# Attention feeding a routed mixture of experts: a new issue order, two packed parameter loads, and the first expert's weight parts moved behind the last route

## The chip, the cores and the metric

The kernel runs on 1 core of one Trainium2 chip. The metric is device time in microseconds (us) of one execution; lower is better. Before the change it is 464.62 us, the median of 3 runs (464.45 to 464.82).

## The reference

Inputs: q, k, v of shape (2 batches, 8 heads, 768 tokens, 64), a hash matrix of 64 x 6, and the experts' weights (8 experts, 512 x 1024 and 1024 x 512).

```
q_bucket, k_bucket = 6 sign bits of q@proj, k@proj, as a number
mask   = q_bucket[:, None] == k_bucket[None, :]
scores = where(mask, q@k.T / 8, -1e9)
attn   = exp(scores - max) / (sum + 1e-9);   x = attn @ v        # (2, 768, 8*64)

for b: for s in order:
    fresh = argmax(x[b,s] @ w_gate)
    e = fresh if s == 0 or sigmoid(x[b,s] @ w_local) < 0.5 else previous e
    p = softmax(x[b,s] @ w_gate)[e]
    out[b,s] = p * (relu(x[b,s] @ w1[e]) @ w2[e])
```

The expert of a token can depend on the token before it, so routing is a scan along the sequence.

## The kernel before

Engine names are those of the profile: PE multiplies matrices, DVE, ACT and POOL work elementwise, SP only starts transfers; POOL and ACT start some too.

**Attention.** Heads go in 8 pairs, p = 0 to 7; pairs 0 to 3 are batch 0. A pair has 12 units `s1` (128 queries by 384 keys: PE products, then a maximum on DVE, L222), which give the row maxima, and 12 units `s2` (128 keys by 384 queries: four products on PE, L213, then exp on ACT, L263, to a tile `pt`). `pv` multiplies `pt` with v (L277), `padd` sums `pt` over key blocks on DVE or POOL (L270). `hash` and `bd` make the bucket bits and put them into the tiles `b` as extra rows; `hi` and `lo` split q and k into a rounded part and the rest (`hx`, `lx`). `ma` to `mf` put the maxima in. `sa`, `sb` (`sah`, `sbh` for half a pair) make the divisors, `ot` copies the result out of PSUM, and `ug` turns it by a product with `iw`, an identity with gate weights beside it (L371), and divides it (L379, L384).

**The order.** `ORDER` is a list written out by hand: each word calls one of these functions, and all engines keep this order within their own queues. `MOVED` says which units sit on a second engine or queue. `busy` is a pair of products on zeros whose result nobody reads. `vsum`, `flat` serve rows whose bucket is empty.

**Routing.** `route` (called through `step`, in parts) runs once for batch 0, then for each half of batch 1. It finds the expert (DVE, L438 to L445, result `rZ`), turns it (PE, L455, tile `tk`), scans along the tokens (DVE, L458, L460), turns the result back (L467, tile `tb`), computes each token's slot `rsi` and probability (L473 to L488), and lets POOL write the tokens' rows into `xs`, a table in DRAM of 256 slots for each expert (L494). Expert 0's inputs don't wait for the table: `xt0` is put together in PSUM by products with one-hot matrices (`oh`, L580; `gather`, L614), from rows read back for batch 0 (`xa`, L588) and from the rounded and rest parts `xhl` of batch 1's first half and `xh`, `xl` of its second half.

**Experts.** `expert` (eight times) loads four parts of w1 and four of w2 of 512 KB each through SP (L644, four buffers `st`), splits each into a rounded part `wh` (ACT, L647) and a rest `wl` (L648), and multiplies (L678, tile `hps`; L696, tile `yps`), three products for each pair. `wl` is made by DVE, for the four w1 parts of expert 0 by POOL. `xprep` loads the next expert's rows `xsl` (L653) and turns them (L657, tile `xps`); `PI` (L629) holds the probabilities and token numbers of expert 0. `overflow_count` counts experts with more than 256 tokens.

Of the kernel before, what the change touches and what calls it, by code (L numbers as in the profile page):

```python
# [22 lines left out]
lx.0.0 busy.2 lx.0.1 busy.2 busy.2 busy.2 lhw busy.2 busy.2 hi.0.1 busy.2 lcs busy.2 lx.1.0 lx.1.1 busy.2 busy.2  # L23
hash.0 hi.0.0 busy.2 ident busy.2 bd.0.1.1 busy.2 hi.1.1 lo.0.1 bd.0.0.1 lo.0.0 busy.2 bd.0.0.0 bd.0.1.0 busy.2
load_v.0.2 busy.2 busy.2 busy.2 hash.1 busy.2 busy.2 s1.0.0.0 busy.2 s1.0.0.1 s1.0.1.0 hi.1.0 lo.1.0 busy.2 lx.2.1
busy.2 s1.0.1.1 bd.1.0.0 busy.2 bd.1.0.1 s1.0.2.0 busy.2 s1.0.2.1 busy.2 busy.2 clear busy.2 busy.2 load_v.0.0
s1.0.3.0 ma.0.0 busy.2 s1.0.3.1 busy.2 busy.2 busy.2 bd.1.1.1 busy.2 mb.0.0 s1.0.4.0 busy.2 lx.2.0 load_v.0.3 s1.0.4.1
s1.0.5.0 bd.1.1.0 busy.2 s1.0.5.1 busy.2 busy.2 mc.0.0 lo.1.1 s2.0.1.0 ma.0.1 s2.0.0.0 s1.1.0.0 hash.2 mb.0.1 busy.2
s1.1.0.1 busy.2 s1.1.1.0 s2.0.2.0 s1.1.1.1 busy.2 load_v.0.5 load_v.0.1 s1.1.2.0 hi.2.1 s2.0.4.0 load_v.0.4 lx.3.0
mf.0.0 mc.0.1 s2.0.3.0 s1.1.2.1 busy.2 s2.0.1.1 bd.2.1.0 s1.1.3.0 s2.0.0.1 busy.2 s1.1.3.1 s2.0.4.1 s1.1.4.0 bd.2.1.1  # L30
busy.2 padd.0.1.0 s2.0.2.1 bd.2.0.1 s1.1.4.1 vsum.0 hi.2.0 s2.0.5.1 s1.1.5.0 s1.1.5.1 pv.0.0.0 bd.2.0.0 mf.0.1
pv.0.1.0 padd.0.1.1 pv.0.0.1 pv.0.1.1 s1.2.0.0 s2.0.5.0 s2.0.3.1 s1.2.0.1 s1.2.1.0 pv.0.2.0 padd.0.2.0 ma.1 lx.3.1 iwc
pv.0.2.1 hash.3 io flat.0.1 flat.0.0 mb.1 s1.2.1.1 padd.0.3.0 padd.0.2.1 s1.2.2.0 s1.2.2.1 hi.3.1 bd.3.0.0 bd.3.0.1
pv.0.3.0 pv.0.3.1 pv.0.4.1 hi.3.0 padd.0.3.1 lo.2.0 padd.0.4.1 mc.1 bd.3.1.1 padd.0.4.0 pv.0.4.0 pv.0.5.1 bd.3.1.0
s1.2.3.0 s2.1.1.0 padd.0.5.1 s2.1.0.0 s1.2.3.1 padd.1.1.0 s2.1.2.0 s2.1.2.1 s1.2.4.0 s2.1.1.1 padd.0.5.0 s2.1.0.1
s2.1.3.0 lo.2.1 s2.1.5.0 s1.2.4.1 padd.1.2.0 lx.4.0 mf.1 pv.0.5.0 s1.2.5.0 padd.1.1.1 s1.2.5.1 s1.3.0.0 ot.0
padd.1.2.1 pv.1.0.1 pv.1.0.0 pv.1.1.0 pv.1.2.0 s1.3.0.1 s2.1.5.1 padd.1.3.0 s2.1.4.1 s1.3.1.0 s2.1.4.0 lx.4.1 s2.1.3.1
load_v.1.3 ma.2 s1.3.1.1 sa.0 padd.1.3.1 hash.4 flat.1.1 flat.1.0 mb.2 sb.0 pv.1.1.1 pv.1.2.1 bd.4.1.0 lo.3.0 pv.1.3.0
pv.1.3.1 padd.1.4.1 s1.3.2.0 s1.3.2.1 lx.5.0 s1.3.3.0 pv.1.4.1 bd.4.0.0 bd.4.0.1 pv.1.4.0 mc.2 pv.1.5.1 pv.1.5.0
s1.3.3.1 hi.4.1 iwl.1 ot.1 s2.2.0.0 padd.1.4.0 s2.2.1.1 s1.3.4.0 lo.3.1 bd.4.1.1 padd.1.5.0 s2.2.2.1 iwl.0 s2.2.1.0  # L40
padd.1.5.1 s1.3.4.1 s1.3.5.0 lx.5.1 pv.2.0.0 s1.3.5.1 s2.2.3.0 hi.4.0 s2.2.3.1 s2.2.2.0 s2.2.0.1 s2.2.4.0 sa.1 ma.3
padd.2.1.0 hash.5 mb.3 padd.2.1.1 sb.1 padd.2.2.0 mc.3 pv.2.0.1 pv.2.1.1 pv.2.1.0 pv.2.2.0 mf.2 pv.2.2.1 s1.4.0.0
# [734 lines left out]
```

## Time and profile before

| | |
|---|---|
| time, median of 3 | 464.62 us (464.45 to 464.82) |
| profiled execution: its own time, its span | 463.13 us, 461.3 us |
| PE busy | 432.1 us, 94% |
| DVE, ACT, POOL busy | 297.3, 203.3, 177.2 us |
| DMA | 60.17 MB, mean 130 GB/s |
| granted PE clock, mean of the span | 0.983 |

Busy time of PE includes ends that are modelled, so a PE that is busy need not run at its peak; what tells is the idle time before an instruction and who ended it (in brackets in the rows below). Span and time differ by what lies before and after the program's instructions. The attention with its routing takes the first 271 us of the span, the experts the rest.

### The profile page before, as it was taken

The page shows a single profiled execution, that of the slowest core. Times are in us where ns is not written, and L with a number is a line of the kernel's source. Part 1 is how long each engine was busy: PE and PEld are TensorE (multiplying, and loading weights), DVE is VectorE, ACT ScalarE, POOL GpSimd, SP SyncE. Part 2 cuts the span into 40 slices and gives each one's busy share as a digit, 9 for nine tenths or more (in the row PEclk, how much of TensorE's full clock was granted, in tenths as well). Part 3 has the DMA queues.
Part 4 walks back from the last instruction along what each step waited for, and adds up shares of the span by engine and source line. Part 5 has one row for each costly group of instructions (what it writes and reads, how often), then busy time and mean ns, then how long its engine had stood idle before and what let it go on. Part 6 is the DMA issues. An engine that isn't in the chain of part 4 may idle for free.

```text
span 461.3 us, 8283 instructions
## 1 busy us (share of the span) xinstructions
PE 432.1 (94%) x3316; PEld 338.3 (73%) x3316; DVE 297.3 (64%) x441; ACT 203.3 (44%) x277; POOL 177.2 (38%) x127
## 2 busy tenths in 40 slices
PE   8989999999999999999988289999999999999993
PEld 7976565765767475566654289899999999998982
DVE  5987794646675768876678977573736473738210
ACT  1133454552726353353355046473736364646210
POOL 4369455388577566165356620101010101010100
PEclk9999999999999999999999599999999999999997
DMA  4532111112040030501156539966766766775000
GB/s 154 158 105 76 51 60 42 43 31 81 1 153 28 2 107 3 184 0 70 48 190 222 182 113 285 327 210 217 230 220 219 219 240 220 234 233 192 36 2 31
DMA packets 41577, 60.17 MB, mean 130 GB/s; under 512 B 5949, under 2 KB 24093, under 8 KB 41536
## 3 DMA queue, kind: packets, MB, share of 16 engines
q1 hardware_dynamic: 38010, 50.54, 34.1%
...
HBM read 47.66 MB, written 11.56 MB: 128 GB/s over the span
## 4 chain that ended last, share of the span: by engine, by line
PE 41%; issue 36%; DVE 12%; POOL 5%; ACT 3%; DMA 2%; POOLq 0%; SPq 0%; DVEq 0%; ACTq 0%
PE s L213 19%; PE pv L277 11%; POOL out L700 4%; PE ug L371 3%; DVE rw L438 3%; PE busy L550 2%; DVE sp L270 2%; ACT pt L263 2%; DVE mx L222 2%; PE hb L181 1%; DMA PI<-xs 1%; DVE lx L205 1%; DMA hw<-proj 1%; DVE rC L460 1%; PE pv L284 1%
## 5 line engine op out<-in xcount | busy, mean ns | idle before, releaser
L222 DVE TENSOR_REDUCE mx<-s 128x2 f32<-128x768 f32 x96 | 88.5, 953 | 41.2 <-PE s L213 40.6
L648 DVE TENSOR_TENSOR wl<-st,wh 128x1024 fp32r<-128x1024 f32 x60 | 71.9, 1220 | 60.7 <-ACT wh L647 60.7
L263 ACT ACTIVATE pt<-s 128x768 f32<-128x768 f32 x96 | 73.2, 811 | 64.8 <-PE s L213 59.6
L270 POOL TENSOR_TENSOR sp<-sp,pt 128x768 f32<-128x768 f32 x42 | 79.5, 1904 | 57.1 <-DVE sp L270 28.7
L647 ACT ACTIVATE wh<-st 128x1024 fp32r<-128x1024 f32 x64 | 66.6, 1059 | 49.3 <-DMA st<-w 29.2
L213 PE MATMUL s<-hx 64*128 64x384 f32 x384 | 71.1, 366 | 3.0 <-DVE mx L222 2.7
L678 PE MATMUL hps<-xH,wh 128*128 128x256 f32 x256 | 70.8, 278 | 0.7 <-ACT xH L711 0.7
L678 PE MATMUL hps<-xH,wl 128*128 128x256 f32 x256 | 70.6, 277 | 0.0
L678 PE MATMUL hps<-xL,wh 128*128 128x256 f32 x256 | 70.4, 277 | 0.0
L700 POOL DMA_INDIRECT out<-y,xsl x14 | 15.3, 1092 | 143.3 <-ACT y L699 143.3
L277 PE MATMUL pv<-pt,v 128*64 128x384 f32 x384 | 68.5, 494 | 0.0
L213 PE MATMUL s<-b,b 64*128 64x384 f32 x384 | 65.1, 334 | 0.0
L213 PEld LDWEIGHTS s<-hx 64*128 64x128 f32 x384 | 36.2, 184 | 26.1 <-issue 8.8
L696 PE MATMUL yps<-wh,hH 128*128 128x512 f32 x128 | 50.6, 395 | 0.0
L696 PE MATMUL yps<-wh,hL 128*128 128x512 f32 x128 | 50.4, 393 | 0.0
L696 PE MATMUL yps<-wl,hH 128*128 128x512 f32 x128 | 50.0, 391 | 0.0
L277 PEld LDWEIGHTS pv<-pt,v 128*64 128x64 f32 x384 | 24.9, 136 | 32.9 <-issue 32.1
L678 PEld LDWEIGHTS hps<-xH,wh 128*128 128x128 f32 x256 | 48.1, 188 | 1.2 <-ACT xH L711 0.9
L678 PEld LDWEIGHTS hps<-xH,wl 128*128 128x128 f32 x256 | 48.1, 188 | 0.3
L678 PEld LDWEIGHTS hps<-xL,wh 128*128 128x128 f32 x256 | 48.0, 188 | 0.0
L213 PEld LDWEIGHTS s<-b,b 64*128 64x128 f32 x384 | 36.4, 185 | 0.4 <-DMA b<-br 0.4
L213 PE MATMUL s<-hx,lx 64*128 64x384 f32 x192 | 32.6, 334 | 0.0
...
## 6 DMA issues: line engine op xcount, KB each, us to landing
...
```

Of the source, the lines that this page charges most:

```text
L213: nc.tensor.matmul(out=sc[:, h, 0:384], lhsT=w[r, cols[0]], rhs=x[r, cols[1]], tile_position=(64 * h, 0), start=first and n == 0, stop=las ...
L222: nc.vector.tensor_reduce(out=MX[p][:, kh, i // 3, :, i % 3], in_=sc[:, :, 0:384], axis=AX.X, op=ALU.max)
L263: nc.scalar.activation(out=pt.rearrange("p (a q) -> p a q", a=2), in_=sc[:, :, 0:384], func=ACTF.Exp, scale=0.125)
L270: eng.tensor_tensor(out=SP[p, h], in0=PT[p, 0, h] if kt == 1 else SP[p, h], in1=PT[p, kt, h], op=ALU.add)
L277: nc.tensor.matmul(out=PV[p][64 * h:64 * h + 64, half, 0:384], lhsT=V[b, kt][:, pp * 128 + 64 * h:pp * 128 + 64 * h + 64], rhs=PT[p, kt, h ...
L371: nc.tensor.matmul(out=t[:, half, j * 146:j * 146 + 146], lhsT=OT[p][:, q * 128:q * 128 + 128], rhs=iw[:, pp])
L438: V_.scalar_tensor_tensor(out=kp, in0=LG[b][:, qr, 8], scalar=0.0, in1=cs[:, 160 + q0:160 + q0 + n], op0=ALU.is_ge, op1=ALU.mult)
L647: nc.scalar.activation(out=H, in_=st, func=ACTF.Copy)
L648: (eng or nc.vector).tensor_tensor(out=L, in0=st, in1=H.bitcast(F32), op=ALU.subtract)
L678: nc.tensor.matmul(out=hps[:, k], lhsT=w[:, c, fs], rhs=x[:, c], start=(n == 0), stop=(n == 11))
L696: nc.tensor.matmul(out=yps, lhsT=h[:, k, ts], rhs=w[:, k], start=(n == 0), stop=(n == 23))
L700: i = nc.gpsimd.indirect_dma_start(out=out, out_offset=bass.IndirectOffsetOnAxis(ap=pi[:, t, 1:2].bitcast(I32), axis=0), in_=y, in_offset= ...
```

## The change

- `ORDER` and `MOVED` are replaced. The units are the same, but 40 words `busy` stand where 44 stood, and their order on every engine is another. Two of the differences that matter below: of the first four loads of q and k, three go out at once (SP: xq, xk; ACT: xk of pair 1), and the fourth, xq of pair 1, goes on SP behind `hw` and `cs`; and two more `s2` units of pair 7 stand ahead of the first half's `ugh`.
- `hw` (hash matrix) and `iw` come ready-made from DRAM, in one load each, in place of a memset and two or three loads.
- The last part of the attention (the gathers of `xt0`) is issued by hand as well; `hle` makes both of its rests on DVE.
- The first expert's `wl` are made by DVE, not by POOL, and held behind the route: the first one behind the last one-hot matrix, the others behind the route's last copy. Its `wh` on ACT are held behind the route's last copy `rK`.
- `overflow_count` is issued after expert 0, and `xsl` of expert 1 is loaded by POOL's queue.

```
-lx.0.0 busy.2 lx.0.1 busy.2 busy.2 busy.2 lhw busy.2 busy.2 hi.0.1 busy.2 lcs busy.2 lx.1.0 ...
+busy.2 busy.2 lx.0.0 lx.0.1 busy.2 busy.2 busy.2 lhw lcs lx.1.0 hi.0.1 lo.0.1 lx.1.1 hi.0.0 ...
...
-            nc.scalar.activation(out=K, in_=tk[0:8, i, 0:384], func=ACTF.Copy)
+            AFTER["ACT"] = nc.scalar.activation(out=K, in_=tk[0:8, i, 0:384], func=ACTF.Copy).ins
...
-        V_.tensor_copy(out=EC[b][:, :, qr], in_=tb...)
+        AFTER["last"] = V_.tensor_copy(out=EC[b][:, :, qr], in_=tb...).ins
...
-    nc.vector.memset(hw, 0.0)
...
     def lhw():
-        for h in range(2):
-            queue("lhw").dma_start(out=hw[64 * h:64 * h + 64, 13 * h:13 * h + 12]...
+        queue("lhw").dma_start(out=hw, in_=proj)
...
-        nc.gpsimd.memset(iw, 0.0)
...
-    def iwl(h): ...
-    def iwc(): ...
+    def iwl():
+        nc.sync.dma_start(out=iw.rearrange("p a c -> p (a c)"), in_=wg)
...
     def onehot(tag, o):
-            nc.vector.tensor_scalar(out=oh[:, j], in0=IO[0], ...)
+            AFTER["first"] = nc.vector.tensor_scalar(out=oh[:, j], in0=IO[0], ...).ins
...
     def hle(i):
-        (nc.gpsimd, nc.vector)[i].tensor_tensor(
+        nc.vector.tensor_tensor(
...
-    overflow_count()
...
-    def weights(src, shape, pool, eng=None):
+    def weights(src, shape, pool, after=None):
...
-        nc.scalar.activation(out=H, in_=st, func=ACTF.Copy)
-        (eng or nc.vector).tensor_tensor(out=L, in0=st, in1=H.bitcast(F32), op=ALU.subtract)
+        with tc.issue_after(after["ACT"]) if after else nullcontext():
+            nc.scalar.activation(out=H, in_=st, func=ACTF.Copy)
+        with tc.issue_after(after.pop("first", after["last"])) if after else nullcontext():
+            nc.vector.tensor_tensor(out=L, in0=st, in1=H.bitcast(F32), op=ALU.subtract)
...
-    def xprep(slots):
+    def xprep(slots, queue=nc.sync):
...
     for e in range(NE):
-        xt = expert(w1[e], w2[e], xt, (lambda: xprep(...)) ..., None if e else nc.gpsimd)
+        xt = expert(w1[e], w2[e], xt, (lambda: xprep(..., nc.sync if e else nc.gpsimd)) ..., None if e else AFTER)
+        if e == 0:
+            overflow_count()
```

POOL, from the rows of batch 0 (`xt_109`) written to the slots to the load of `PI`, before; `xl` are rests of batch 1's second half:

```order
L494 DMA xs<-xt_109,rsi 2048x514 x6
L356 TENSOR_TENSOR xl<-xt_110,xh 128x3x128 x3
L494 DMA xs<-xt_110,rsi 2048x514 x3
L595 TENSOR_TENSOR xhl<-xt_110,xhl 128x768
L648 TENSOR_TENSOR wl<-st,wh 128x1024 x4
L494 DMA xs<-xt_110,rsi 2048x514 x3
L629 DMA PI<-xs 128x2x2
```

and now (L623 is `PI`, L648 is now `xsl`):

```order
L356 TENSOR_TENSOR xl<-xt_110,xh 128x3x128
L270 TENSOR_TENSOR sp<-sp,pt 128x768
L356 TENSOR_TENSOR xl<-xt_110,xh 128x3x128
L494 DMA xs<-xt_109,rsi 2048x514 x6
L494 DMA xs<-xt_110,rsi 2048x514 x3
L356 TENSOR_TENSOR xl<-xt_110,xh 128x3x128
L494 DMA xs<-xt_110,rsi 2048x514 x3
L623 DMA PI<-xs 128x2x2
L648 DMA xsl<-xs 128x2x514
```

The rest `xhl` and the four `wl` have left POOL, the three `xl` are spread, and `xsl` stands behind `PI`.

DVE, from the last copy back (`ec`) of the last route on, before (`RK` feeds the one-hot matrices; `OV`, `ni`, `bt` belong to `overflow_count`):

```order
L470 COPY ec_121<-tb 128x24
L510 COPY OV<-to 128x17
L471 TENSOR_TENSOR RK<-tb,ec_121 128x3
L473 TENSOR_TENSOR rt_3101<-tb,cs 128x24
L580 TENSOR_SCALAR oh<-io,RK 128x256 x3
L474 SCALAR_TENSOR_TENSOR rt_3101<-rt_3101,tb 128x24
```

and now, with the first `wl` (L643) behind the one-hot matrices (L573):

```order
L470 COPY ec_121<-tb 128x24
L471 TENSOR_TENSOR RK<-tb,ec_121 128x3
L573 TENSOR_SCALAR oh<-io,RK 128x256 x3
L473 TENSOR_TENSOR rt_3079<-tb,cs 128x24
L643 TENSOR_TENSOR wl<-st,wh 128x1024
L474 SCALAR_TENSOR_TENSOR rt_3079<-rt_3079,tb 128x24
```

DVE, from the last sum of the last route into the first expert, before, where the two halves of `xL` (L712) take rests of w2 between them:

```order
L516 TENSOR_REDUCE bf_3232<-bt_3231 1x5
L487 TENSOR_TENSOR xt_110<-rpr,rse 128x3
L517 CAST be<-bf_3232 1x5
L712 TENSOR_TENSOR xL<-xt_3113,xH 128x512
L648 TENSOR_TENSOR wl<-st,wh 128x1024
L712 TENSOR_TENSOR xL<-xt_3113,xH 128x512
L648 TENSOR_TENSOR wl<-st,wh 128x1024 x3
```

and now, where the first half of `xL` (L707) stands inside the route and the second behind the second `wl`:

```order
L486 TENSOR_REDUCE rpr<-rt_3080 128x3
L707 TENSOR_TENSOR xL<-xt_3091,xH 128x512
L487 TENSOR_TENSOR xt_110<-rpr,rse 128x3
L488 COPY ec_121<-tb 128x2x24
L491 COPY cnt_3187<-rC 8x1
L643 TENSOR_TENSOR wl<-st,wh 128x1024
L707 TENSOR_TENSOR xL<-xt_3091,xH 128x512
L643 TENSOR_TENSOR wl<-st,wh 128x1024 x3
```

The column `xt_110` that L487 writes is what the last three writes to the slots (L494) wait for. On PE the first expert's products start now with eight of the first w1 part, then seven of the second, and only then those that read the second half of `xL`.

## Rows read from the trace of the kernel before

**Rows 1.** Busy time by stretch: window, PE, PEld, DVE, ACT, POOL, clock, DMA, GB/s.
```profile
22.00:45.00 23.00, 21.62 (x207) 16.44 (x203) 18.57 (x26) 9.13 (x12) 16.85 (x13) 1.00 0.29 90
45.00:70.00 25.00, 23.87 (x201) 15.37 (x201) 21.95 (x27) 10.68 (x15) 12.40 (x7) 1.00 0.16 51
145.00:170.00 25.00, 24.21 (x202) 15.53 (x201) 16.30 (x28) 11.59 (x17) 16.46 (x12) 1.00 0.14 49
170.00:195.00 25.00, 23.06 (x198) 15.65 (x196) 20.52 (x34) 10.42 (x15) 11.64 (x7) 1.00 0.24 87
245.00:270.00 25.00, 14.46 (x97) 11.30 (x92) 21.48 (x51) 6.84 (x11) 15.19 (x9) 0.80 0.45 159
285.00:461.00 176.00, 168.37 (x1099) 152.42 (x1097) 89.39 (x91) 84.47 (x105) 17.58 (x16) 0.99 0.58 190
```
**Rows 2.** DVE in order of time, L438: start, duration, idle before in brackets.
```profile
233.93 0.15 DVE L438 SCALAR_TENSOR_TENSOR rw<-lg,cs 128x3 f32<-128x3 f32 x1
...
250.28 10.67 DVE L438 SCALAR_TENSOR_TENSOR rw<-lg,cs 128x3 f32<-128x3 f32 x1
```
**Rows 3.** POOL in order of time, the same stretch.
```profile
250.00 1.75 POOL L595 TENSOR_TENSOR xhl<-xt,xhl 128x768 fp32r<-128x768 f32 x1
251.69 9.23 POOL L648 TENSOR_TENSOR wl<-st,wh 128x1024 fp32r<-128x1024 f32 x4
```
**Rows 4.** PE in order of time, from the last route to expert 0's turn of xsl.
```profile
261.97 0.80 PE L455 MATMUL tk<-cs,rZ 128*8 128x128 f32 x3 [9.30 <-DVE rZ L445]
...
271.32 0.38 PE L678 MATMUL hps<-xH,wh 128*128 128x256 f32 x1 [0.75 <-ACT xH L711]
...
282.75 1.04 PE L657 MATMUL xps<-cs,xsl 128*128 128x128 f32 x8
```
**Rows 5.** Busy time by stretch, around that wait (columns of rows 1).
```profile
250.00:262.00 12.00, 2.39 (x20) 1.98 (x19) 11.93 (x10) 1.69 (x3) 10.92 (x5) 0.69 0.45 158
262.00:266.00 4.00, 4.00 (x25) 3.70 (x25) 3.32 (x10) 0.48 (x1) 0.00 (x0) 0.66 0.37 129
```
**Rows 6.** Chain of waits, the start: start, duration, what held it.
```profile
2.46 4.71 DMA hw<-proj
```
**Rows 7.** PE in order of time, the start.
```profile
1.78 5.36 PE L550 MATMUL busy<-Fl 64*128 64x384 f32 x40 [1.78 <-DVE Fl L538]
```
**Rows 8.** DVE and POOL in order of time, pair 7's second half.
```profile
235.34 3.75 DVE L270 TENSOR_TENSOR sp<-pt 128x768 f32<-128x768 f32 x1 [0.29 <-ACT pt L263]
239.20 0.96 DVE L270 TENSOR_TENSOR sp<-sp,pt 128x768 f32<-128x768 f32 x1
...
235.60 2.67 POOL L356 TENSOR_TENSOR xl<-xt,xh 128x384 fp32r<-128x384 f32 x3
```
**Rows 9.** Chain of waits: two s2 units on PE.
```profile
29.38 1.39 PE s L213 x16
```
**Rows 10.** DVE in order of time, the last route and expert 0's xL.
```profile
266.33 0.18 DVE L470 COPY ec<-tb 128x24 f32<-128x24 f32 x1 [0.17 <-PE tb L467]
...
266.80 0.15 DVE L471 TENSOR_TENSOR RK<-tb,ec 128x3 f32<-128x3 f32 x1
...
271.30 0.69 DVE L712 TENSOR_TENSOR xL<-xt,xH 128x512 fp32r<-128x512 f32 x1 [2.23 <-ACT xH L711]
```
**Rows 11.** Costliest groups of instructions: busy, mean ns, idle before.
```profile
L648 DVE TENSOR_TENSOR wl<-st,wh 128x1024 fp32r<-128x1024 f32 x60 | 71.9, 1220 | 60.7 <-ACT wh L647 60.7
```
**Rows 12.** POOL in order of time, the last writes to the slots and PI.
```profile
271.84 0.97 POOL L494 DMA_INDIRECT xs<-xt,rsi  x1 [0.30 <-issue]
276.53 0.76 POOL L629 DMA_DIRECT2D PI<-xs  x1 [3.72 <-DMA xs<-xt,rsi]
```
**Rows 13.** Chain of waits: from PI's issue to its landing.
```profile
276.53 5.13 DMA PI<-xs
```
**Rows 14.** The tile xsl: from issue to landing, all seven loads by SP.
```profile
DMA to landing us min/median/max: 2.5/3.3/7.0
```
**Rows 15.** Busy time by stretch, while POOL issues PI (columns of rows 1).
```profile
274.00:278.00 4.00, 4.00 (x36) 4.00 (x35) 4.00 (x5) 2.38 (x4) 0.76 (x1) 1.00 0.67 168
```

More of the change, by code (lines that the diff above doesn't have):

```diff
@@ L1 @@
-from contextlib import ExitStack
+from contextlib import ExitStack, nullcontext
 import numpy as np
@@ L22 @@
 ORDER = """
[L23 to L42, printed above, removed]
@@ L68 @@
-pv.7.2.1 padd.7.3.1 s2.7.4.1 s2.7.5.1 step split_l.2 split_l.0 xa.1 split_l.1 flat.7.1 step hle.0 hle.1 pv.7.3.1
-sah.7.1 pv.7.4.1 ohe pv.7.5.1 oth.7.1 sbh.7.1 ugh.7.1 split_h.3 step split_l.3
+busy.2 busy.2 lx.0.0 lx.0.1 busy.2 busy.2 busy.2 lhw lcs lx.1.0 hi.0.1 lo.0.1 lx.1.1 hi.0.0 busy.2 busy.2 hash.0
+busy.2 busy.2 load_v.0.1 bd.0.0.1 busy.2 hi.1.1 bd.0.1.0 ident lo.0.0 busy.2 busy.2 bd.0.0.0 busy.2 lo.1.1 bd.0.1.1
+busy.2 busy.2 hash.1 hi.1.0 busy.2 busy.2 lx.2.0 lx.2.1 busy.2 busy.2 s1.0.0.0 busy.2 bd.1.1.1 load_v.0.3 s1.0.0.1
@@ L599, in tile_kernel @@
     parts = {f.__name__: f for f in (
-        bd, busy, clear, fill_slots, fill_some, flat, hash, hi, hle, ident, io, iwc, iwl, lcs, lhw, lo, load_v, lx,
+        bd, busy, clear, fill_slots, fill_some, flat, hash, hi, hle, ident, io, iwl, lcs, lhw, lo, load_v, lx,
         ma, mb, mc, mf, ohe, ot, oth, padd, pv, s1, s2, sa, sah, sb, sbh, split_h, split_l, step, ug, ugh, vsum, xa)}
-    with tc.manual_schedule():
-        for part in ORDER.split():
-            part, *where = part.split(".")
-            parts[part](*map(int, where))
-    xt0 = pvp.tile([128, 4, 256], F32, tag="pv", name="xt0")
-    x2 = xt0.rearrange("p (b c) n -> p b (c n)", b=2)
-    for i in range(2):
-        nc.tensor.matmul(out=x2[:, i], lhsT=zr, rhs=Fl[0:1, 0:512], start=True, stop=False)
     def gather(oh, hl, c0, c1, last=False):
@@ L662, in xprep, with expert @@
         return xsl[:, :, 512:514], xH, xL
-    def expert(w1e, w2e, xt, mid=None, eng=None):
+    def expert(w1e, w2e, xt, mid=None, after=None):
         pi, xH, xL = xt
@@ L667, in expert @@
         w2v = w2e.rearrange("(f p) c -> p f c", p=128)
-        W1 = [weights(w1v[:, :, 256 * i:256 * i + 256], [128, 4, 256], w1p, eng) for i in range(4)]
+        W1 = [weights(w1v[:, :, 256 * i:256 * i + 256], [128, 4, 256], w1p, after) for i in range(4)]
         hs = []
@@ L759 @@
     B, H, S, D = inputs["q"].shape
+    hw, iw = np.zeros((128, 32), np.float32), np.zeros((128, 4, 146), np.float32)
+    g = np.concatenate([inputs["moe_w_gate"], inputs["moe_w_local"]], axis=1).reshape(4, 2, D, 9)
+    iw[:, :, 0:128] = np.eye(128)[:, None]
+    for h in range(2):
+        r = slice(64 * h, 64 * h + 64)
+        hw[r, 13 * h:13 * h + 12] = np.tile(inputs["proj"], (1, 2))
+        iw[r, :, 128 + 9 * h:137 + 9 * h] = g[:, h].transpose(1, 0, 2)
     arrays = {
```

127 lines of the change are left out of this document (74 added, 53 removed), and 8 rows, old and new, of the table MOVED.

## The prediction, made before the run

> **What bounds the kernel now.** I read four views, in this order. The busy times by stretch say which engine has no room: the reader is to see that PE has idle time of only 1.38 us in the stretch from 22 to 45 us, 1.13 from 45 to 70, 0.79 from 145 to 170 and 1.94 from 170 to 195, and then, all at once, some ten of 25 us from 245 on [rows 1]. From 285 us to the end PE is busy 168.4 of 176 us; it is the bound of the experts, so whatever starts them later or makes PE wait in them moves the end by as much [rows 1]. The second view, PE in order of time, names the gap: PE waits 9.30 us for DVE's `rZ` of the last route, and expert 0 starts at 271.32 us [rows 4]. The third, DVE in order of time, says why: one small instruction of the route (L438) took 10.67 us, where the same one took 0.15 us a route earlier [rows 2]. The fourth, POOL in order of time, says whom it waited for: it began 0.28 us after POOL had begun `xhl`, POOL then ran the four `wl` without a pause, and both ended together (251.69 + 9.23 = 260.92 and 250.28 + 10.67 = 260.95 us) [rows 2, 3]. DVE had waited for POOL's elementwise work on SBUF, not for data. In the same gap the granted clock fell: 0.69 and 0.66 in the means of the next stretches, that is the lower level of 1.2 GHz for part of them [rows 5].
>
> **The change part by part.** The sum is made against the profiled execution's own 463.13 us, which is 1.49 us under the median of 464.62.
>
> *The wait at L438.* With `xhl` and the four `wl` off POOL, nothing but one short `xl` and transfers' issues are left there. The instruction should take 0.15 us again: gain 10.5 us. If POOL's remaining `xl` (a third of 2.67 us [rows 8]) falls upon it, 0.9 us of that are lost.
>
> *The clock.* Without the long gap I expect the full 2.4 GHz. At 0.66 of it, PE's `tk` took 0.80 us [rows 4, 5] and should take some 0.5; with a little for the gathers I count 0.5 us gained (bounds 0 and 1).
>
> *overflow_count.* Its copies stood on DVE between the scan and the one-hot matrices: `RK` began 0.47 us after `ec` [rows 10], with one of them in between. 0.4 us gained; they now stand among expert 0's rests of weights, where DVE has waits to spare [rows 11].
>
> *The first `wl` on DVE.* Here the change costs something, since DVE is now on the way into expert 0. Call X the moment when the first half of `xH` is ready (271.3 before). Before, all of `wl` was there, and 96 products ran from 271.32 to 282.75 without a gap, 0.119 us each [rows 4]. Now DVE makes the first `wl` (1.22 us [rows 11]) while PE gathers, which hides it; but behind it come ten small instructions of the route, so the first half of `xL` ends at about X + 1.0, not X + 0.7 (its own 0.69 us [rows 10]). PE's first eight products end at X + 1.7. The seven of the second part need the second `wl`: X + 1.0, three small instructions of 0.15 us each, 1.22 us, together X + 2.7; PE is through with them at X + 3.5, the second half of `xL` is there at X + 3.4, and the other 81 products take 9.6 us: X + 13.1 in place of X + 11.4. Loss 1.7 us (bounds 0.7, if the route's instructions fit before X, and 3).
>
> *`xsl` behind `PI` on POOL.* PE turns it right after those 96 products. The last three writes to the slots wait for L487, which now stands behind the first half of `xL`: X + 1.2, and with the lag to POOL X + 1.5. They are issued 1.27 us apart (0.97 and 0.30 [rows 12]), the last at X + 4.0. From the last one's issue to `PI` it was 4.69 us [rows 12], so `PI` is issued at X + 8.7 and `xsl` at X + 9.5. SP's loads of it landed after 2.5 to 7.0 us [rows 14], `PI` itself on POOL's queue after 5.1 [rows 13]. Nearest is `PI`; for 514 KB in place of 2 KB I take 6 us: X + 15.5 against X + 13.1, so PE waits 2.4 us (bounds 0 and 3.5). Nothing later gives it back, since PE has no slack there [rows 1]. While POOL issued `PI`, DVE was busy 4.00 of 4 us and the issue took 0.76 us [rows 12, 15]: it was not held up visibly.
>
> *The start.* The first hash product waited 4.71 us for `hw` [rows 6], which queues behind 384 KB loads; four of these were under way, now three are ahead of it. A quarter of 4.71 is 1.2 us. PE has 28 products on zeros ahead of the hash, not 40, at 5.36/40 us each [rows 7]: 1.6 us less, so they don't stand in the way. I take 1.1 us (bounds 0 and 1.6).
>
> *Pair 7's second half.* DVE's first sum took 3.75 us where the next took 0.96, beside three `xl` of 2.67 us on POOL [rows 8]: the same wait as at L438, on the way to the scan. The `xl` are spread now: gain 2.8 us. Against it two more `s2` units stand before the first half's `ugh`: 1.39 us [rows 9]. Net 1.4 us (bounds -1.5 and 2.8). The six writes of batch 0's rows to the slots come later, and `xa`, read back from them, with them; I expect it just in time and keep 1.5 us of the lower bound for it.
>
> *The rest of the order.* PE work is the same but for 16 products on zeros. What a new order can win is PE's idle time in the four stretches above, 1.38 + 1.13 + 0.79 + 1.94 = 5.2 us; it can also lose. I take 1.5 us, some three tenths, with bounds of 5.2 on both sides. This is the least certain term. The ready-made `iw` takes loads off SP and a memset off POOL, far from where they are used: nothing.
>
> Sum: 10.5 + 0.5 + 0.4 - 1.7 - 2.4 + 1.1 + 1.4 + 1.5 = 11.3 us. 463.13 - 11.3 = 451.8 us for an execution like the profiled one, and with 1.49 us back, 453.3 us for the median.
>
> **The rivals.**
>
> *Late `xsl` and a slow clock.* If `xsl` lands at its upper bound, or POOL's issue of it is held up by DVE's `wl`, PE waits 3.5 us or more, and the clock may fall, as in the 9.30 us gap [rows 4, 5]. What the two stretches of rows 5 lost to the clock, 0.31 x 12 + 0.34 x 4 = 5.1 us of full speed, is its price if PE is busy all that time. Against it: shorter gaps went without a fall (clock 1.00 in the stretches from 22 to 195 us [rows 1]), and `PI`'s issue was not held up. 453.3 + 1.1 + 5.1 = 459.5 us. The Trainium skill, SBUF — State Buffer, section "SBUF: two separate sides", warns of just this pair: a transfer issued from GpSimd can be starved of descriptors while VectorE runs an instruction in a two-port mode, 620 ns becoming some 3100 by its figures. By that rule alone, without the clock, `xsl` would land some 2.5 us later and the result would be an estimated 456 us; the 0.76 us of `PI`'s issue beside a busy DVE speak against it.
>
> *The order wins more.* The idle time of the four stretches goes nearly all (3.7 us more than counted) and `xsl` is in time (2.4): 447.2 us. For it: PE's waits there are short and many, which is what an order can mend; against it: any order has DVE reduce, ACT exponentiate and PE multiply the same units.
>
> *Weights late.* The buffers `st` came free when POOL made `wl`, by 260.9 us, X - 10 [rows 3]; now the last one comes free at about X + 6.7, and the fourth part of w2 is loaded only then. At 190 GB/s [rows 1] 512 KB take 2.8 us, rounding and rest 2.3 more: X + 11.8, before its use. If loads crowd and take twice as long, the whole of expert 0 and 1 runs behind them by some 5 us: 458 us.
>
> *Slower than before.* DVE's sums and splits of two SBUF tiles wait whole POOL instructions out, as the 2.8 us in rows 8. The units move, and POOL's and DVE's shares stay alike, so such meetings will come at other places. Where they hit the maxima of `s1`, for which PE waits, each costs PE up to 2.8 us. Five more than now in pairs 1 to 6 eat the gain (5 x 2.8 = 14 against 11.3); with five the time is 453.3 + 14 = 467 us. Against it: there are about as many such sums and splits on either engine as before, so that many more meetings on PE's way would be chance.
>
> *It does not do what it says.* Another instruction of POOL holds L438, or the route waits elsewhere for as long: 464.6 us.
>
> **How the numbers follow.** Forecast 0.55 (453.3 us, own range 450 to 456.5); order wins more 0.15; late `xsl` with slow clock 0.15; weights late 0.08; no effect 0.03; slower 0.04. About 0.2% (0.9 us) is what a measurement of this kernel can tell from no change. Faster: 0.55 + 0.15 + 0.15 + 0.08 = 0.93; same 0.03; slower 0.04. The range reaches from 448 to 459.5 us; outside lie the slower cases, the one without effect and part of the fastest.
>
> **What would show it.** Right: L438 under 1.2 us in the last route; no PE wait over 2 us for `rZ`; clock 1.00 around it; the first hash product near 6.2 us; expert 0's first product near 261 us. For the costs: two waits of PE in its first 15 products, for `xL` and for the second `wl`, and one of about 2.4 us before `xps`. Wrong: DVE again in one small instruction for microseconds while POOL runs; expert 0 starting at 261 us but the end not earlier by as much, with waits for `wh` or `wl`; or PE idle in pairs 1 to 6 by more than the 5.2 us of before.

## The result, and the profile after

The changed kernel takes 458.43 us (median of 4 runs, 458.17 to 461.59) against 464.72 us; the ratio is 0.9877 (95% interval 0.9851 to 0.9904). That is faster, as forecast, but by 6.3 us where 11.3 were forecast. The time lies inside the stated range (448 to 459.5 us) and outside the forecast's own (450 to 456.5 us). Two rivals stand near it, "weights late" (458 us) and "late `xsl` and a slow clock" (459.5 us): the time alone does not tell them apart, the trace has to.

| | before | after |
|---|---|---|
| profiled execution: own time, span | 463.13, 461.3 us | 458.60, 456.8 us |
| PE busy | 432.1 us | 431.3 us |
| DVE, ACT, POOL busy | 297.3, 203.3, 177.2 us | 284.7, 205.6, 171.9 us |
| X, first half of `xH` ready | 271.3 us | 253.6 us |
| first product of expert 0, of expert 1 | 271.3, 294.6 us | 254.6, 289.0 us |

Expert 0 starts 16.7 us earlier, expert 1 only 5.7 us. The busy times by stretch (columns as in [rows 1]) show where:

```profile
22.00:45.00 23.00, 21.53 (x199) 16.27 (x201) 15.25 (x22) 11.86 (x16) 12.29 (x9) 1.00 0.21 61
45.00:70.00 25.00, 25.00 (x218) 15.92 (x215) 18.97 (x29) 13.90 (x21) 18.18 (x10) 1.00 0.29 95
145.00:170.00 25.00, 25.00 (x209) 15.69 (x210) 17.31 (x29) 10.58 (x15) 11.13 (x9) 1.00 0.08 22
170.00:195.00 25.00, 25.00 (x216) 17.33 (x216) 18.79 (x29) 11.50 (x16) 21.55 (x12) 1.00 0.02 4
245.00:270.00 25.00, 17.64 (x147) 16.80 (x144) 18.28 (x37) 12.66 (x16) 10.07 (x8) 0.96 0.80 254
270.00:285.00 15.00, 9.93 (x41) 8.45 (x42) 8.89 (x10) 8.12 (x10) 1.02 (x2) 0.72 0.83 285
285.00:457.00 172.00, 163.79 (x1075) 148.42 (x1073) 83.76 (x89) 78.68 (x98) 16.61 (x16) 0.99 0.55 179
```

In the three stretches between 45 and 195 us that are shown, PE's idle time (1.13, 0.79 and 1.94 us before) is gone; from 22 to 45 us it is 1.47 us, where it was 1.38. The gap now lies between 245 and 285 us, where DMA moves 254 to 285 GB/s and the clock falls to a mean of 0.72. DVE in order of time, the last route, answers [rows 2]:

```profile
242.57 0.15 DVE L438 SCALAR_TENSOR_TENSOR rw<-lg,cs 128x3 f32<-128x3 f32 x1
...
246.85 1.58 DVE L460 TENSOR_TENSOR_SCAN rC<-rE,rC 8x384 f32<-8x384 f32 x1
```

L438 takes 0.15 us and comes 7.7 us earlier. PE in order of time answers [rows 4]:

```profile
244.77 0.49 PE L455 MATMUL tk<-cs,rZ 128*8 128x128 f32 x3
...
254.62 0.36 PE L673 MATMUL hps<-xH,wh 128*128 128x256 f32 x1 [1.75 <-DVE cnt L491]
...
275.07 1.94 PE L652 MATMUL xps<-cs,xsl 128*128 128x128 f32 x8 [9.20 <-DMA xsl<-xs]
```

The wait of 9.30 us for `rZ` is gone, and one of 9.20 us for `xsl` has come. What `xsl` waited for stands on POOL (answers [rows 12]):

```profile
254.64 1.89 POOL L494 DMA_INDIRECT xs<-xt,rsi  x1 [7.03 <-DVE cnt L491]
256.83 3.68 POOL L494 DMA_INDIRECT xs<-xt,rsi  x1 [0.31 <-issue]
260.82 0.97 POOL L494 DMA_INDIRECT xs<-xt,rsi  x1 [0.30 <-issue]
268.76 0.76 POOL L623 DMA_DIRECT2D PI<-xs  x1 [6.97 <-DMA xs<-xt,rsi]
269.50 0.77 POOL L648 DMA_DIRECT2D xsl<-xs  x1
```

and DVE beside it:

```profile
254.45 1.20 DVE L643 TENSOR_TENSOR wl<-st,wh 128x1024 fp32r<-128x1024 f32 x1
255.58 0.67 DVE L707 TENSOR_TENSOR xL<-xt,xH 128x512 fp32r<-128x512 f32 x1
256.19 3.47 DVE L643 TENSOR_TENSOR wl<-st,wh 128x1024 fp32r<-128x1024 f32 x3
259.59 0.67 DVE L678 SCALAR_TENSOR_TENSOR hL<-hps,hH 128x512 fp32r<-128x512 f32 x1
```

The writes of tokens' rows to the slots (L494, `DMA_INDIRECT`) are called scatters from here on, and the making of a `wl` a split. The first two scatters end 0.88 and 0.85 us after the `wl` beside them end (255.65 and 259.66 us). The third, with no split beside it, takes 0.97 us as before. The list of DMA issues gives the median us from issue to landing, here of one transfer each (the third scatter, and the load of `xsl`):

```profile
xs<-xt,rsi POOLq DMA_INDIRECT x1, 7.7
xsl<-xs POOLq DMA_DIRECT2D x1, 514.0 KB, 5.4
```

Before, the last scatters landed 3.2 to 5.0 us after their issue. A held scatter was in the trace of before as well, between two that were not held: one of the first half's began while DVE made the rest `xhl` and ended 0.84 us after it.

```profile
246.90 0.96 DVE L595 TENSOR_TENSOR xhl<-xt,xhl 128x768 fp32r<-128x768 f32 x1 [1.23 <-ACT xhl L594]
...
247.13 1.57 POOL L494 DMA_INDIRECT xs<-xt,rsi  x1 [0.30 <-PE pv L277]
```

X, the end of the first `xH`, is read from ACT, before and after:

```profile
270.67 0.60 ACT L711 ACTIVATE xH<-xt 128x512 fp32r<-128x512 f32 x1 [7.38 <-PE xt L614]
...
252.97 0.60 ACT L706 ACTIVATE xH<-xt 128x512 fp32r<-128x512 f32 x1 [0.37 <-PE xt L599]
```

The wait for `xsl` hides a second bound. ACT and DVE make `hH` and `hL` for the products behind it, and splits that waited for loads stand among these: the fourth part of w2 is rounded only from 267.06 us on, and its `wl` ends at X + 15.8, where the prediction had X + 11.8. Two parts of expert 1's w1 follow. So the last `hL` that expert 0 needs ends at 273.2 us, 1.9 us before PE goes on:

```profile
267.06 1.06 ACT L641 ACTIVATE wh<-st 128x1024 fp32r<-128x1024 f32 x1 [1.95 <-DMA st<-w]
...
272.52 0.68 DVE L678 SCALAR_TENSOR_TENSOR hL<-hps,hH 128x512 fp32r<-128x512 f32 x1
```

### The profile page after: what moved, and what is told of

The parts are those of the page before. It is cut to its first block, busy times and chain, and to the rows that moved or that the text cites. A ratio compares the mean times of both kernels' runs of the same rounds, so it can differ in the third digit from the quotient of the medians.

```text
span 456.8 us, 8266 instructions
## 1 busy us (share of the span) xinstructions
PE 431.3 (94%) x3300; PEld 337.6 (74%) x3300; DVE 284.7 (62%) x445; ACT 205.6 (45%) x278; POOL 171.9 (38%) x121
## 4 chain that ended last, share of the span: by engine, by line
PE 52%; issue 38%; POOL 5%; DVE 2%; DMA 1%; ACT 1%; POOLq 0%; SPq 0%; ACTq 0%
PE s L213 23%; PE pv L277 15%; POOL out L695 4%; PE busy L549 4%; PE ug L371 3%; PE hb L181 1%; PE st L329 1%; POOL xs L494 1%; PE xt L599 1%; PE pv L284 1%; PE st L338 1%; DVE sp L270 1%; PE xt L614 0%; PE st L300 0%; PE vt L527 0%
## 5 line engine op out<-in xcount | busy, mean ns | idle before, releaser
L643 DVE TENSOR_TENSOR wl<-st,wh 128x1024 fp32r<-128x1024 f32 x64 | 76.8, 1221 | 63.2 <-ACT wh L641 63.0
L270 POOL TENSOR_TENSOR sp<-sp,pt 128x768 f32<-128x768 f32 x41 | 76.9, 1886 | 44.4 <-DVE sp L270 34.9
L277 PE MATMUL pv<-pt,v 128*64 128x384 f32 x384 | 69.7, 495 | 0.0
L213 PEld LDWEIGHTS s<-hx 64*128 64x128 f32 x384 | 36.4, 184 | 23.4 <-issue 7.2
```

The costliest lines, as they stand in the source:

```text
L213: nc.tensor.matmul(out=sc[:, h, 0:384], lhsT=w[r, cols[0]], rhs=x[r, cols[1]], tile_position=(64 * h, 0), start=first and n == 0, stop=las ...
L270: eng.tensor_tensor(out=SP[p, h], in0=PT[p, 0, h] if kt == 1 else SP[p, h], in1=PT[p, kt, h], op=ALU.add)
L277: nc.tensor.matmul(out=PV[p][64 * h:64 * h + 64, half, 0:384], lhsT=V[b, kt][:, pp * 128 + 64 * h:pp * 128 + 64 * h + 64], rhs=PT[p, kt, h ...
L643: nc.vector.tensor_tensor(out=L, in0=st, in1=H.bitcast(F32), op=ALU.subtract)
```

## The experiments

Theory A: DVE's splits stretch the issue of the scatters. Theory C: the weights' loads, which now run beside the scatters, make their landing late. Theory B: the load of `xsl` itself is late because POOL issues it. Times are medians; ratios are to the kernel before, on the same chip.

| run | us | ratio (95%) |
|---|---|---|
| low parts left out | 456.34 | 0.9803 (0.9739 to 0.9867) |
| later weight loads left out | 453.75 | 0.9731 (0.9696 to 0.9765) |
| slots turned late | 457.65 | 0.9833 (0.9805 to 0.9861) |
| old order, new place of `wl` | 459.61 | 0.987 (0.983 to 0.991) |
| `xsl` on SP | 455.82 | 0.9788 (0.976 to 0.9816) |
| new order, `wl` on POOL | 466.18 | 1.0014 (0.9977 to 1.0052) |
| a quarter of the bytes | 457.49 | 0.9826 (0.9784 to 0.9868) |
| combined | 452.96 | 0.9744 (0.9717 to 0.9771) |
| old order, tail of combined | 461.49 | 0.994 (0.9908 to 0.9972) |
| combined, turn ahead | 454.56 | 0.977 (0.9736 to 0.9805) |
| combined, other banks | 454.30 | 0.9758 (0.973 to 0.9786) |

**Low parts left out.**

```
         H = pool.tile(...);  L = pool.tile(...)
         ... wh ...
+        if drop: return H, H        # expert 0: w1 parts 1 to 3, all of w2
```

> The changed kernel, with seven of the first expert's eight low weight parts left out (parts 1 to 3 of w1 and all of w2 use the high part twice; the products stay, their number too). In the changed kernel the last three scatters take 1.89, 3.68 and 0.97 us on POOL, land 7.6 to 8.8 us after their issue, and TensorE waits 9.2 us for the slots of expert 1. Theory A (VectorE's large SBUF operations beside them stretch the writing of the scatters): all three take 1.0 us, 1.27 apart, the last is issued near 257.2 instead of 260.8; if they land 4.4 us later as before, the slots are there near 266 to 268, the wait is 0 to 2.5 us and the time 447 us (444.5 to 450). Theory C (the transfers compete with the loads of the weights, which fill the DMA engines from 240 us on): even where the issue gets shorter, each lands 7 to 8.5 us after it; wait 5 to 7 us, time 453 to 456 us. Theory B (what is late is the load of the slots itself, on POOL's queue behind PI): the landing 5.4 us after its issue stays, and with the scatters as late as now the time stays at 458 us.

```profile
254.97 0.99 POOL L494 DMA_INDIRECT xs<-xt,rsi  x1 [7.39 <-DVE cnt L491]
256.27 0.97 POOL L494 DMA_INDIRECT xs<-xt,rsi  x1 [0.30 <-issue]
257.55 0.97 POOL L494 DMA_INDIRECT xs<-xt,rsi  x1 [0.30 <-issue]
265.27 0.76 POOL L623 DMA_DIRECT2D PI<-xs  x1 [6.75 <-DMA xs<-xt,rsi]
```

Without splits beside them the scatters take 0.97 us each, and `PI` is issued 3.5 us earlier: A holds for the issue. The last one still lands 7.4 us after its issue, so A is not all. PE waits 3.67 us for `xsl` instead of 9.20, between A's 0 to 2.5 and C's 5 to 7. That wait is shorter than it would be at full speed: the clock's mean was 0.67 from 255 to 260 us, so the products with w1 ended later too (267.66 us, where the changed kernel's ended at 265.87).

**A quarter of the bytes.**

```
-        nc.sync.dma_start(out=st, in_=src)
+        nc.sync.dma_start(out=st[:, 0:1, 0:256], in_=src[:, 0:1, 0:256])
         # wh and wl read this quarter four times
```

> The changed kernel in which each weight load brings a quarter of its tile (128 KB instead of 512), and the splits on ACT and DVE read that quarter four times: as many loads, splits and products of the same size, a quarter of the bytes. VectorE's splits still stand beside the last three scatters. Theory A alone (VectorE stretches the writing of the scatters, the loads don't matter): 1.9 and 3.7 us on POOL as now, landing 7.6 to 8.8 us after the issue, wait for the slots 7 to 9 us, time 457 us. Theory C (the loads compete with the transfers): landing 2 to 4.7 us after the issue as before the change, the last by 263 to 265.5, the slots by 267 to 269; wait 1 to 3.5 us; time 450 us (447 to 453). Both (what the run without the low parts suggests, where the scatters took 0.97 us each and still landed 7.7 us after their issue): issue stretched, landing fast, time as under C.

POOL, and then the landing of the third scatter:

```profile
256.07 1.90 POOL L494 DMA_INDIRECT xs<-xt,rsi  x1 [8.07 <-DVE cnt L491]
258.27 3.68 POOL L494 DMA_INDIRECT xs<-xt,rsi  x1 [0.30 <-issue]
262.25 2.01 POOL L494 DMA_INDIRECT xs<-xt,rsi  x1 [0.30 <-issue]
```

```profile
xs<-xt,rsi POOLq DMA_INDIRECT x1, 4.2
```

The issue is stretched as ever; this time the third one too, since a `wl` began 0.06 us ahead of it (262.19 to 263.42 us; the scatter ends 0.84 us later). The landing is back to 4.2 us. The scatters of the first half, at 243 to 247 us, show C by itself, since no split stood beside them: 0.97 to 0.98 us of issue in both kernels, but 6.6 to 7.3 us to the landing in the changed kernel and 3.1 to 3.5 here. So both are at work, each on its own part of the way: A on the issue, C on the landing. The time was off: 457.5 us, not 450. The third scatter lost another 1 us, and `xsl` took 6.4 us to land. SP had started the 514 KB of expert 2's slots at 266.55 us, just ahead of it (267.50); that this made it late is not shown, since in the next run the same load stood as close ahead of an `xsl` that took 5.2. PE still waited 6.38 us.

**Later weight loads left out.**

```
+        W1 = KEEP if KEEP else [weights(...) ...]      # every expert: expert 0's w1
+        W2 = [... views of W1 ...]
```

> The changed kernel with all weight loads but the first expert's w1 left out (every expert multiplies by that w1, also in place of w2), and so their splits on ACT and DVE. In the stretch of the last scatters, the first expert's w1 parts are still split on DVE, but no weight load runs beside the transfers. Theory A: the scatters still take 1.9 and about 2 to 3 us on POOL, because the splits of w1 stand beside them; they land 7 us or more after their issue, as now; wait of TensorE for the slots 6 to 9 us. Theory C: whatever their issue takes, they land 3.2 to 4.7 us after it, as before the change, and the slots land under 3.5 us after their issue; wait 0 to 4 us. With both at work: issue stretched, landing fast, wait about 2 to 4 us. The whole time is read only for the stretch up to the first expert's end; if TensorE's clock stays up it is 445 to 452 us.

This did not test what it was made for. Three of the four loads of w1 began at 255.3 us instead of 240, probably because with fewer tiles the buffers `st` lay in memory that the attention held longer; so they ran beside the scatters after all, and the first product waited for them:

```profile
258.27 0.58 PE L673 MATMUL hps<-xH,wh 128*128 128x256 f32 x1 [3.05 <-ACT wh L641]
```

Two things can be read from it. No split stood beside the scatters, and they took 0.99, 0.97 and 0.97 us, as A has it. And from 265 us on no weights were loaded, only expert 2's slots by SP, and `xsl` on POOL's queue still took 5.2 us to land.

**`xsl` on SP.**

```
-xprep(xs[...], nc.sync if e else nc.gpsimd)
+xprep(xs[...], nc.sync)
```

> The changed kernel with one argument undone: the slots of expert 1 are loaded by SP's queue, as before, not by POOL's behind PI. On SP this load stands behind the first expert's w2 and ahead of expert 1's w1, so SP stands there until the scatters have landed, and expert 1's w1 is loaded behind it. Theory B (POOL's queue makes the load of the slots late): it lands 2.5 to 3.5 us after its issue instead of 5.4; with the scatters as late as now the wait of TensorE is 6 us instead of 9.2, time 455 us. Theory C (weight loads beside the transfers): expert 1's w1 no longer loads beside the scatters, so the last one lands by 264 to 266 instead of 268.5 and the slots by 267 to 269; wait 1 to 3.5 us, time 452 us (449.5 to 455), less if expert 1's w1 is then what is late. If neither queue nor loads matter and only VectorE's work beside the scatters does (A): wait 8 to 9 us, time 457.5 to 459 us.

```profile
273.25 1.94 PE L652 MATMUL xps<-cs,xsl 128*128 128x128 f32 x8 [3.28 <-DMA xsl<-xs]
```

SP started `xsl` at 269.20 us, so it landed within 4.05 us, against 5.2 to 7.3 on POOL; and with expert 1's w1 loaded behind it, the last scatter landed 5.8 us after its issue, not 7.7. So C has a part in the scatters; for `xsl` itself the run does not tell the other queue (B) from the loads that no longer stand ahead of it. In this profiled execution X came 2.5 us later than in the changed kernel's, at a clock of 0.72 in the stretch from 250 to 262 us; this execution was the slowest of six (458.89 us), and the wait of 3.28 us is again shortened by products with w1 that took 12.9 us instead of 11.3. The median, 455.8 us, lies above C's range and nearer to B's 455.

**Slots turned late.**

```
         xsl = mp.tile(...);  queue.dma_start(out=xsl, ...)     # xprep: the load, as now
+        return lambda: xsplit(xsl)                             # turn and split: later
...
             OC.append(i)
+            if mid and after and t == LATE:                    # expert 0, LATE = 1
+                nxt = nxt()
```

> The changed kernel, the slots of expert 1 loaded where they are now, but turned by TensorE behind the first expert's 48 products with w2 instead of ahead of them. Nothing of the scatters or loads changes, so they land when they do now (268.5 and 274.9). If the wait for the slots is what the tail lost, TensorE goes from the last product with w1 (near 265.9) into those with w2: it waits in pieces for the low parts and w2 (DVE finishes the fourth hL at 273 behind splits that wait for weight loads), 2 to 5 us in all, and then 1 to 2 us for the split of the slots; time 451 us (448 to 454), 4 to 10 us under the changed kernel. If the loads of the weights are the bound of this stretch whatever TensorE does (rival), the w2 products wait for them as long as the turn did, and the time is 456 to 459 us.

PE's waits behind the products with w1:

```profile
271.52 0.50 PE L696 MATMUL yps<-wh,hH 128*128 128x512 f32 x1 [1.00 <-ACT hH L680]
273.07 0.50 PE L696 MATMUL yps<-wh,hL 128*128 128x512 f32 x1 [0.82 <-DVE hL L681]
284.14 0.39 PE L676 MATMUL hps<-xH,wh 128*128 128x256 f32 x1 [3.18 <-ACT xH L658]
```

A miss: 457.65 us, not 451. The long wait is gone, but `hH` and `hL` stood on ACT and DVE behind splits of expert 1's w1 that waited for loads, the split of the slots now lay bare (3.18 us, part of it behind a split of weights that waited for its load), and expert 1's products with w1 ran 13.2 us (284.14 to 297.36) instead of the changed kernel's 11.3, at a clock of 0.50 from 286 to 288.5 us. The rival (loads bind the stretch) was nearer: with the wait for `xsl` out of the way, the time fell by 0.8 us only.

**The two halves of the change, each alone.** Old order with the new place of `wl`:

```
 # kernel before, and in weights():
+        with tc.issue_after(after["ACT"]): ... wh on ACT
+        with tc.issue_after(after.pop("first", after["last"])): ... wl on DVE
```

> The kernel before, old order, old loads, gather and overflow count as they were; changed only where the low parts of the first expert's w1 are made (VectorE, the first behind the one-hots, the rest behind the last route; their high parts on ACT behind the last copy of the route). The 10.67 us in which VectorE waited at the last route's first instruction go away. Theory A and C both: part of it is given back in the tail, where the scatters stand beside VectorE's splits and the weight loads: wait for the slots 3 to 8 us instead of none. Time 458.5 us (456 to 462). If nothing is given back: 454 us. If the whole gain of the change came from the order: 464 us.

```profile
249.97 1.36 DVE L438 SCALAR_TENSOR_TENSOR rw<-lg,cs 128x3 f32<-128x3 f32 x1
251.25 0.16 DVE L439 TENSOR_REDUCE rmx<-lg 128x3 f32<-128x24 f32 x1
```

L438 now waits only for POOL's `xhl` (249.55 to 251.30 us), which this version keeps. X is 262.9 us, 8.4 earlier than before. The scatters are stretched here too (1.73, 2.01 and 0.97 us). 459.61 us is within 1.2 of the changed kernel. The number came, its reason did not: the wait of 3 to 8 us for the slots, which was to eat the gain, was not there.

```profile
274.83 1.06 PE L659 MATMUL xps<-cs,xsl 128*128 128x128 f32 x8
```

Of the 8.4 us at X, 7.2 are left at expert 1's first product (287.40 against 294.63 us) and 4.3 at the end; the rest is lost in expert 1, which takes 24.1 us instead of 22.8, and later.

New order with `wl` on POOL:

```
-        with tc.issue_after(...): ... wh
-        with tc.issue_after(...): nc.vector.tensor_tensor(out=L, ...)
+        ... wh;  (eng or nc.vector).tensor_tensor(out=L, ...)     # POOL for expert 0
```

> The changed kernel with the new place of the first expert's low w1 parts undone: POOL makes all four, as before, and their high parts are not held; order and loads stay new. On POOL they stand ahead of the last three scatters (9.2 us of work, from about 247.6). If POOL's large subtractions again hold a VectorE instruction until they are through (10.5 us before the change), the last route stands from about 248 to 257 and the gather comes up to 8 us later: time 464 us (461 to 466), the order by itself worth about nothing. If VectorE's small instructions pass beside them, the gather is where it is now, the scatters go from 257 to 261 without being stretched, and the time is 456 us (454 to 458).

ACT in order of time:

```profile
247.13 1.06 ACT L640 ACTIVATE wh<-st 128x1024 fp32r<-128x1024 f32 x1 [8.22 <-DMA st<-w]
248.10 0.83 ACT L587 ACTIVATE xhl<-xt 128x768 fp32r<-128x768 f32 x1
```

466.18 us: the number was right, the reason only in part. A `wh` that nothing held stood on ACT ahead of the second `xhl`, waited 8.22 us for its load, and DVE waited 8.7 us for `xhl`. Behind that, POOL's `wl` stretched DVE, as expected:

```profile
248.39 7.79 POOL L641 TENSOR_TENSOR wl<-st,wh 128x1024 fp32r<-128x1024 f32 x3
251.52 5.08 DVE L573 TENSOR_SCALAR oh<-io,RK 128x256 fp32r<-128x256 f32 x3
```

The one-hot matrices (L573) take 0.88 us in the changed kernel. With `xhl` (2.63 us, 0.95 there) and the scan `rE` (2.64 us, 1.01 there) the stretch comes to some 7.5 us. In this form the new order brought nothing.

**Combined.** Three edits on the changed kernel:

```
+xprep(xs[...], nc.sync)                                   # xsl by SP, behind w2
...
+            if mid and pi is PI and t == LATE:                # expert 0, LATE = 0
+                nxt = nxt()                                   # turn between the halves of w2
...
+            HELD["ACT"] = nc.scalar.activation(out=hH, ...).ins
+            HELD["last"] = nc.vector.scalar_tensor_tensor(out=hL, ...).ins
+    xt = expert(..., (AFTER, HELD)[e] if e < 2 else None)     # expert 1's w1: wh, wl behind these
```

> A version meant to keep what the tail gave back. Against the changed kernel: the slots of expert 1 loaded by SP behind the first expert's w2; TensorE turns them between the two halves of the w2 products instead of ahead of both; the split of expert 1's w1 on ACT and DVE held behind the first expert's last hH and hL, which now stand behind splits that wait for weight loads. From the trace: products with w1 254.7 to 266, first half with w2 to 271.5, turn to 273, second half to 278.6, expert 1 from 279 instead of 289. If nothing else is late: 448.5 us. With 1 to 4 us of new waits (expert 1's w1 lands by about 276): 451 us (448 to 454.5), the forecast. If the loads of the weights bound this stretch whatever the order (rival), 455 to 458 us.

Busy times by stretch, around the former gap:

```profile
262.00:275.00 13.00, 13.00 (x89) 11.90 (x88) 7.40 (x12) 6.26 (x8) 1.26 (x2) 1.00 0.80 266
275.00:290.00 15.00, 15.00 (x106) 13.74 (x105) 11.98 (x16) 11.33 (x13) 2.57 (x2) 1.00 0.94 321
```

PE is busy throughout, the clock is 1.00, expert 1 starts at 280.6 us. 452.96 us is in the expected range, 2 us above the figure given, and under both kernels. The scatters are still stretched (1.89 and 3.68 us), but PE no longer waits for what stands behind them. Not all is at full speed: the clock's mean is 0.66 from 255 to 260 us, so that expert 1 starts 26.3 us after X (23.4 before the change), and it takes 24.3 us itself instead of 22.8.

**Combined, turn ahead.** One of the three edits undone, the place of the turn:

```
-            if mid and pi is PI and t == LATE:
-                nxt = nxt()
+        if mid:
+            nxt = nxt()              # ahead of both halves
```

> The combined version with one of its three edits undone: TensorE turns the slots of expert 1 ahead of both halves of the w2 products again. Slots loaded by SP behind w2 and expert 1's w1 split held, as in it. The scatters land near 266, the slots near 270; the products with w1 end near 266 to 268. Theory (the turn has to stand where its data is there): TensorE waits 2 to 4 us for the slots and the clock may fall behind it; time 455 us (453.5 to 457.5). If the place of the load and of the splits was all that mattered: 453 us.

```profile
270.82 1.94 PE L655 MATMUL xps<-cs,xsl 128*128 128x128 f32 x8 [5.12 <-DMA xsl<-xs]
```

PE waits 5.12 us, more than expected, and the clock's mean is 0.66 from 265 to 275 us. 454.56 us as expected, but its interval meets the combined version's: the edit's worth in time is not settled.

**Old order, tail of combined.** The three edits on the run of the old order with the new place of `wl` (`xsl` is on SP there already).

> The old order (kernel before, with the first expert's low parts on VectorE, as in the run of that half alone, 459.6 us), and now also the mended tail of the combined version: slots of expert 1 loaded by SP behind w2 (as in the kernel before), turned between the two halves of the w2 products, split of expert 1's w1 held behind the first expert's last hH and hL. With the new order and this tail the time was 453.0 us; the new order brings the first expert's start 8.6 us earlier (254.3 against 262.9). If that head start comes through once the tail holds nothing back, this run is 6 to 8 us above it: 459 us (457 to 461). If the new order is worth nothing and the tail is all: 453 to 455 us.

461.49 us, 0.5 above the range. In the old order the mended tail wins nothing (459.61 without it). There PE mostly stands from 287.5 to 290 us (busy 0.50 of 2.5): expert 1's `xH` waits on ACT behind a split that waited 2.24 us for its load. The clock falls behind that (mean 0.53 from 292.5 to 295 us), and expert 1's products with w1 run 13.8 us. In the new order the tail wins 5.5 us. With the mended tail the new order is worth 8.5 us (461.49 - 452.96), with the changed kernel's tail 1.2 us (459.61 - 458.43; the intervals overlap). The 8.5 hold that this tail suits the old order badly: each order with the better of its two tails, it is 6.7 us (459.61 - 452.96). These medians come from different chips, where the kernel before takes 464.4 to 465.4 us; "order" means all of the change but the new place of `wl`.

**Combined, other banks.**

```
-    ph = ...tile_pool(name="ph", bufs=4, space=PSUM...);  py = ...
+    py = ...;  ph = ...
```

> The combined version, with the pools of the two kinds of accumulators in PSUM allocated in the other order, so that the first expert's first product doesn't write the bank that the last route's transposed ranks still stand in (read by the copy at L488, which comes behind the first xL on VectorE). If this is what the first product waits 1.75 us for, it starts some 0.8 to 1 us earlier, and the time is 452 us (450 to 453.5); the trace tells it rather than the time. If it waits for the first xL or the second low part (rival), the wait stays 1.75 us and the time 453 us.

```profile
253.61 0.39 PE L676 MATMUL hps<-xH,wh 128*128 128x256 f32 x1 [0.75 <-ACT xH L713]
```

The first product comes 0.04 us behind X instead of 1.05, so it was the bank that the copy at L488 still read. The median shows no gain (454.30 against 452.96 us, intervals overlapping): here expert 1 starts at 279.2 us instead of 280.6, but takes 25.7 us to expert 2's first product instead of 24.3, with waits of 0.52 and 0.53 us before it and PE busy 13.19 of 15 us from 275 to 290. The us is given back.

## Why the prediction was right in its sign and wrong in its size

*L438, `overflow_count`.* Right: 0.15 us. `xl` did not fall upon L438, but on the scan `rC` (1.58 us instead of 1.0). `RK` now begins 0.22 us after `ec` instead of 0.47: 0.25 us, where 0.4 were counted.

*The start.* Forecast 1.1 us; the first hash product came at 6.01 instead of 7.31 us: 1.3. The size is right, the reading was not: 4.71 us is the time of the load of `hw` itself. PE was busy on zeros until 7.14 us and then waited 0.17 us for `hw`. Now the first hash product stands right behind the 28 products on zeros, so how much came from fewer of these and how much from an earlier `hw` is not separated.

*Pair 7 and the rest of the order.* Forecast 1.4 + 1.5 us. Mis-sized to the good side: X came 17.7 us earlier (271.27 to 253.57), where the terms ahead of X gave 15.4 (10.5 + 0.5 + 0.4 + 1.1 + 1.4 + 1.5). The 2.3 us more have two parts. L438 came 7.7 us earlier, where start, pair 7 and order gave 4.0: 3.7 more. From L438 to X it is 11.0 us instead of 21.0, where 11.4 were to be gained and 10.0 were: 1.4 less, 0.6 of it the scan `rC`. PE's idle time in the three stretches from 45 to 195 us went wholly.

*The first `wl` on DVE.* Forecast X + 13.1 for the end of the 96 products; they ended at X + 12.3. The cost is another: the first product came 1.05 us behind X, because of the bank (shown), and the two waits that I named behind it did not come.

*`xsl` behind `PI`: the term that was mis-sized.* Forecast: last scatter issued at X + 4.0, `PI` 4.7 us later, `xsl` landed at X + 15.5, a wait of 2.4 us. Measured: X + 7.25, 7.9 us later, X + 21.4, 9.2 us. Two parts of the sum were each 3.3 us too small. I took the scatters' issue at 0.97 us each from [rows 12], where only the third had a split beside it, begun after it; here it is 1.89 and 3.68 us (that the splits do it is shown by the run without the low parts). The held scatter of 1.57 us in the same trace I had overlooked. I took the way to `PI` from the same rows, where few loads ran; here they do, and it is 7.9 us (that the loads do it is shown by the run with a quarter of the bytes). The landing of `xsl` itself, taken at 6 us, was 5.4; but the bounds of 2.5 to 7.0 us from [rows 14] were no bounds of it. Those are landings of POOL's result scatters, which read `xsl`; the trace has none for SP's loads.

*The clock.* Forecast a gain of 0.5 us. The wait for `rZ` and its slow clock went (`tk` takes 0.49 us instead of 0.80); the wait for `xsl` brought another (mean 0.72 from 270 to 285 us), and turn and products with w2 took 13.9 instead of 11.9 us.

*The sum.* From X to expert 1's first product it was 23.4 us before and 35.4 after: 12.0 lost, where I had counted 4.1 (1.7 + 2.4): of the 12.0, 0.8 are the products with w1 and the wait ahead of them, 9.2 the wait for `xsl`, 2.0 the slow clock behind it. Later stages lose 1.1 more. 17.7 - 12.0 - 1.1 = 4.6 us, the difference of the two profiled executions (4.5); the medians differ by 6.3.

*The rivals.* "Late `xsl` and a slow clock", which had 0.15, is the one that came in its mechanism. That its number (459.5 us) is near is partly luck: its wait of 3.5 us was 9.2, its 5.1 us for the clock were 2.0, and X came 2.3 us earlier than counted. What DVE held was not the issue of `xsl`, as the rival had it (0.77 us), but the scatters ahead of it. I had weighed it down by the 0.76 us of `PI`'s issue beside a busy DVE [rows 12, 15]. That row is true and does not bear on the matter: `PI` is a plain load, and plain loads were not held in any run here, while the scatters, which read their rows' numbers from SBUF, were (that this is the reason is not shown). In the changed kernel `PI` was issued at 268.76 us, in the middle of this split, again in 0.76 us:

```profile
268.15 1.23 DVE L643 TENSOR_TENSOR wl<-st,wh 128x1024 fp32r<-128x1024 f32 x1 [1.54 <-ACT wh L641]
```

The Trainium skill, SBUF — State Buffer, section "SBUF: two separate sides", had a warning near this one; its case is a two-port copy, with 620 ns growing to some 3100, while the splits are subtractions of two SBUF tiles (`tensor_tensor`), and of `tensor_tensor` it says that in a probe it did not stall a DMA. Here such subtractions did hold the scatters, with 0.97 us growing to 3.68: the measurement decides, and that the mechanism is that of the page's copy is not shown. By that rule without the clock I had put `xsl` 2.5 us later; the load itself was not held (0.77 us). "Weights late" (0.08) is not what PE's long wait names, but it stood right behind it: with the turn of the slots moved out of the way the time fell by 0.8 us only, since `hH` and `hL` stood behind splits that waited for loads. And what the loads crowd out first is the scatters. What no run separates is how much of the landing of `xsl` is POOL's queue and how much the traffic beside it.
